# Gates behind the norms in odd MLP blocks, and the first MLP weight in three loads

## Chip, cores, metric

One core of one Trainium2 chip. The metric is the device time of one execution in microseconds. "The span" is the profiled time from the first to the last instruction; it is about 1.8 us shorter than the time of the same run.

## The reference

The result is a gated sum of two branches over 2048 tokens of width 512:

```python
g = sigmoid((x * gate_w).sum(-1, keepdims=True))
a = A(x, mem0, Wq, Wk, Wv, Wo)      # 64 segments of 32 tokens, 32 heads, 8 memory rows carried from segment to segment
y = layernorm(x)
b = gelu(y @ w1 + b1) @ w2 + b2     # w1: 512 x 1376, w2: 1376 x 512
return g * a + (1 - g) * b
```

Only `g` and `b` are touched. The recurrent branch `a` takes the last 87% of the time and stays as it is.

## The kernel before

The kernel computes the whole MLP branch first (about the first 100 us), then the recurrent loop. The 16 tiles of 128 tokens go through the MLP in 8 blocks of two tiles; a block has 11 column blocks `fc` of w1 (ten of 128 columns, one of 96). The loads are queued by SyncE in this order:

```python
ld_x(0, 1); ld_x(1, 2)
nc.sync.dma_start(w1_sb[:, :, 0:3 * P], w1_src[:, :, 0:3 * P])       # 384 KB
ld_x(2, 4)
ld_w2(0, 4)
nc.sync.dma_start(w1_sb[:, :, 3 * P:F], w1_src[:, :, 3 * P:F])       # 992 KB
ld_w2(4, FCF)                                                        # 768 KB
# ... the tail of w2, b2, m0 ...
ld_x(4, 8)                                                           # x of tiles 4 to 7
# ... then Wv, x of tiles 8 to 15, Wq, Wk, Wo
```

`bn(T)` makes mean and variance of a tile on VectorE, `newton` the reciprocal roots, `norm(T)` the normalised tile, `norm_tr(T)` transposes it on TensorE into PSUM bank 7 and copies it out on VectorE (`yT`). `gates(T, T+1)` is the product with `gate_w` and its row sum, on VectorE; `gates2` takes a tanh of the sums on ScalarE and two affine steps on VectorE. `up` is the product with w1 and a GELU on ScalarE; `down` follows two steps later with w2, and its last step evicts the bank (copies it out of PSUM), scaled by `1 - g`:

```python
for u in range(NBLK * FC):
    blk, fc = divmod(u, FC)
    T1 = (blk + 1) * TB                      # first tile of the next block
    pend.append((u, up(u)))
    if fc == 2:
        c_act()                              # ScalarE: eviction of the last block's odd tile, scaled by 1 - g
    if len(pend) > LAG:
        down(*pend.pop(0))                   # at fc == 1 also the VectorE eviction of the last block's even tile
    if T1 < NT:
        if fc == 1 or fc == 3:
            ys[fc // 2] = norm(T1 + fc // 2)
        elif fc == 5 or fc == 7:
            norm_tr(T1 + fc // 2 - 2, ys[fc // 2 - 2])
    if blk % 2 == 0:
        if fc in (2, 5, 6, 7) and T1 + 2 < NT:
            bn(T1 + 2 + (2, 5, 6, 7).index(fc) )
        if fc == 8 and T1 + 2 < NT:
            newton(T1 + 2, T1 + 6)
    elif fc in (2, 4, 6, 8):
        T = T1 + (fc - 2) // 2
        if T < NT:
            gates(T, T + 1)
    elif fc == 10 and T1 < NT:
        gates2(T1, T1 + 4)
    if blk == 0 and fc in (9, 10):
        gates(fc - 9, fc - 8)
    if blk == 1 and fc == 0:
        gates2(0, 2)
    if blk == 1 and fc in (1, 3):
        gates(2 + fc // 2, 3 + fc // 2)
    if blk == 1 and fc == 9:
        gates2(2, 4)
    # ...
```

Instructions of one engine run in this program order. So in block 0 VectorE meets `bn(4)` (at `fc == 2`), which needs the late x load, before `norm(3)`, before the copies of both transposes, and before the gates of tiles 0 and 1.

## Time and profile before

| | |
|---|---|
| time, median of 4 runs | 822.30 us (822.12 to 822.76) |
| profiled run, span | 822.27 us, 820.5 us |
| TensorE idle, whole span | 27.2 us |
| of that, waits between 7.16 and 100 us | 1.18 us for w1, 1.14 us for a GELU |
| first exponential of the recurrent loop | starts at 104.93 us |

How to read it: TensorE has work nearly all the time, so a change pays only if it removes a TensorE wait, or work at half clock, and no later wait grows by as much. The start of the loop's first exponential is a clean mark for that: everything this change can do has happened by then. The views themselves are shown in the prediction.

### The profile page before, as it was taken

How to read it: one execution, taken by the hardware profiler on the slowest of the kernel's cores; microseconds unless marked ns; L12 is line 12 of the kernel's file. 1: busy time of each engine (PE TensorE's matmuls, PEld its weight loads, DVE VectorE, ACT ScalarE, POOL GpSimd, SP SyncE). 2: the span in 40 equal slices, each digit the busy share in tenths (PEclk: the TensorE clock that was granted, in tenths of full speed). 3: DMA queues.
4: the chain of work that ended last, by engine and by line, in shares of the span. 5: the costliest groups of instructions: out<-in, count | busy, mean ns of one | idle time of the engine just before them, and what ended most of it. 6: DMA issues, size and time to landing. Idle time of an engine off the chain costs nothing.

```text
span 820.5 us, 48437 instructions
## 1 busy us (share of the span) xinstructions
PE 793.3 (97%) x22013; PEld 443.2 (54%) x22013; DVE 493.0 (60%) x1022; ACT 446.2 (54%) x1239; POOL 272.1 (33%) x624
## 2 busy tenths in 40 slices
PE   6999999999999999999999999999999999999986
PEld 4666545555555555555555555555555555555543
DVE  5764256565656666665656565656666565656554
ACT  3555545655455555555555655555555556565552
POOL 8100223242434233333424242433333242424220
PEclk9999999999999999999999999999999999999999
DMA  9791310000000010101010100001010101010000
GB/s 315 232 406 53 104 30 10 25 15 17 24 22 25 16 30 10 37 11 36 3 39 8 31 16 22 25 18 28 10 37 10 36 4 41 5 33 8 10 5 24
DMA packets 38357, 37.59 MB, mean 46 GB/s; under 512 B 13561, under 2 KB 36578, under 8 KB 36610
## 3 DMA queue, kind: packets, MB, share of 16 engines
q1 hardware_dynamic: 38018, 34.31, 12.6%
q8 instruction: 174, 2.85, 1.4%
q14 instruction: 37, 0.30, 0.1%
q0 software_dynamic: 128, 0.13, 0.1%
HBM read 26.03 MB, written 6.29 MB: 39 GB/s over the span
## 4 chain that ended last, share of the span: by engine, by line
PE 93%; DVE 3%; DMA 1%; issue 1%; SPq 1%; ACT 1%; DVEq 0%; ACTq 0%
PE b L212 34%; PE b L234 18%; PE b L223 16%; PE b L399 5%; PE b L471 4%; PE b L488 4%; PE b L361 3%; PE b L375 2%; PE b L366 2%; PE b L384 2%; PE b L404 1%; DMA Wo_sb<-in_A_x_dram 1%; PE b L388 0%; DVE R L692 0%; DVE hT L721 0%
## 5 line engine op out<-in xcount | busy, mean ns | idle before, releaser
L218 DVE STREAM_TRANSPOSE Tt<-b 128x512 f32<-128x512 f32 (+1 forms) x384 | 225.6, 613 | 81.6 <-PE b L212 69.0
L212 PEld LDWEIGHTS <-hT 128*32 128x32 bf16 x5120 | 131.0, 97 | 108.5 <-DVE hT L721 23.5
L234 PE MATMUL b<-Wo_sb,UTT 128*32 128x512 bf16 (+1 forms) x2656 | 161.0, 378 | 1.3 <-ACT UTT L763 0.9
L223 PE MATMUL b<-Wv_sb,hT 128*32 128x512 bf16 x2048 | 141.8, 378 | 0.0
L212 PE MATMUL b<-Wq_sb,hT 128*32 128x512 bf16 x2048 | 133.3, 380 | 3.1 <-DVE hT L721 1.7
L212 PE MATMUL b<-Wk_sb,hT 128*32 128x256 bf16 (+1 forms) x3072 | 133.3, 308 | 0.0
L667 ACT CAST KT<-Tt 128x256 bf16<-128x256 f32 (+1 forms) x192 | 87.1, 476 | 53.5 <-DVE Tt L218 53.5
L620 POOL TENSOR_TENSOR Px<-E,R 128x256 bf16<-128x256 bf16 x63 | 42.4, 674 | 209.2 <-DVE R L704 209.2
L704 DVE RECIPROCAL R<-b 128x256 f32<-128x256 f32 x63 | 110.7, 1757 | 0.0
L667 POOL CAST QT<-Tt 128x512 bf16<-128x512 f32 x64 | 39.1, 611 | 187.1 <-DVE Tt L218 187.1
L234 PEld LDWEIGHTS <-UTT 128*32 128x32 bf16 x2656 | 64.4, 96 | 63.7 <-DVE UTT L703 12.1
L711 ACT CAST wsb<-b 128x512 bf16<-128x512 f32 x63 | 36.9, 585 | 111.3 <-PE b L234 111.3
L692 DVE RECIPROCAL R<-b 128x64 f32<-128x64 f32 x63 | 35.1, 557 | 78.6 <-PE b L361 78.6
L634 ACT CAST UTT<-b 128x256 bf16<-128x256 f32 x248 | 74.4, 387 | 9.9 <-PE b L404 8.0
L667 ACT CAST QT<-Tt 128x512 bf16<-128x512 f32 x64 | 39.6, 619 | 68.5 <-DVE Tt L218 68.5
L223 PEld LDWEIGHTS <-hT 128*32 128x32 bf16 x2048 | 49.3, 96 | 21.3
L721 DVE CAST hT<-b 128x32 bf16<-128x32 f32 x63 | 12.0, 191 | 78.8 <-PE b L366 78.8
L476 ACT ACTIVATE hg<-b,b_sb 128x256 bf16<-128x256 f32 x80 | 37.7, 473 | 39.6 <-PE b L471 39.6
L399 PEld LDWEIGHTS <-V 32*128 32x128 bf16 x4064 | 34.4, 91 | 45.5 <-DVE Pm L695 32.2
L471 PE MATMUL b<-yT,w_sb 128*128 128x256 bf16 (+1 forms) x352 | 54.7, 281 | 2.8 <-DMA w_sb<-in_B_w_dram 1.2
L703 ACT CAST UTT<-b 128x64 bf16<-128x64 f32 x126 | 20.6, 215 | 66.1 <-PE b L404 66.1
L622 POOL TENSOR_TENSOR racc<-racc,R 128x320 f32<-128x320 f32 x63 | 54.7, 869 | 0.0
(131 smaller groups left out, 1056.2 us busy)
## 6 DMA issues: line engine op xcount, KB each, us to landing
Wv_sb<-in_A_Wv_dram SPq DMA_DIRECT2D x4, 1024.0 KB
Wq_sb<-in_A_Wq_dram SPq DMA_DIRECT2D x4, 1024.0 KB
Wk_sb<-in_A_Wk_dram SPq DMA_DIRECT2D x4, 1024.0 KB
Wo_sb<-in_A_Wo_dram SPq DMA_DIRECT2D x2, 2048.0 KB
vd<-vt SPq DMA_DIRECT2D x32, 128.0 KB
vs<-vd SPq DMA_DIRECT2D x256, 16.0 KB
out_dram<-o SPq DMA_DIRECT2D x15, 128.0 KB
Wo_sb<-in_A_x_dram SPq DMA_DIRECT2D x1, 1024.0 KB
```

The lines of the kernel that those rows point to most:

```text
L212: nc.tensor.matmul(bk[32 * j:32 * j + 32, 0:n], lhsT=G[:, kc, :], rhs=W5[t][:, kc, h0:h1, j, :], start=(kc == 0), stop=(kc == KC - 1), til ...
L218: nc.vector.transpose(out=Tt[:, 0:n], in_=bk[:, 0:n])
L223: nc.tensor.matmul(bk[32 * j:32 * j + 32, :], lhsT=G[:, kc, :], rhs=Wv5[:, kc, 4 * vb:4 * vb + 4, j, :], start=(kc == 0), stop=(kc == KC - ...
L234: nc.tensor.matmul(bk[32 * g:32 * g + 32, :], lhsT=ut[:, i, j, c0:c0 + 32], rhs=Wo_sb[:, 4 * i + j, d0:d1], start=(j == 0 and i < 4), stop ...
L399: nc.tensor.matmul(U[j][:, i, :], lhsT=V[q, i, :], rhs=Pt[q, i, c_main:c_main + n], start=(i == 0), stop=False, skip_group_check=True, til ...
L471: nc.tensor.matmul(hp[:rows, :], lhsT=w1_sb[:, kc, fc * P:fc * P + rows], rhs=yTs[blk][:, kc, :], start=(kc == 0), stop=(kc == KC - 1))
L476: nc.scalar.activation(out=hg_[:rows, :], in_=hp[:rows, :], func=ACTF.Gelu_apprx_tanh, bias=b1_sb[:rows, fc:fc + 1], scale=1.0)
L620: nc.gpsimd.tensor_tensor(out=Px[:, :, 0:32], in0=E[:, :, 16:48], in1=Rr, op=ALU.mult)
L622: nc.gpsimd.tensor_tensor(out=racc[:], in0=racc[:], in1=R[:], op=ALU.add)
L634: nc.scalar.copy(out=UTT[T % 2][:, :, j, c0 + M:c0 + 40], in_=U[:])
L667: (nc.gpsimd.tensor_copy if bi == 2 else nc.scalar.copy)(out=dst, in_=Tv)
L704: nc.vector.reciprocal(out=R[:, 8 * NG:].rearrange("p (i q) -> p i q", q=32), in_=sr)
```

## The change

The intent: w1's late columns come in two loads, so that the fourth column block need not wait for the last; and in odd blocks the gates stand behind both norms and transposes, so that they can't hold up the next block's input.

```diff
-    nc.sync.dma_start(w1_sb[:, :, 3 * P:F], w1_src[:, :, 3 * P:F])
+    nc.sync.dma_start(w1_sb[:, :, 3 * P:6 * P], w1_src[:, :, 3 * P:6 * P])
+    nc.sync.dma_start(w1_sb[:, :, 6 * P:F], w1_src[:, :, 6 * P:F])
@@ the loop
-        elif fc in (2, 4, 6, 8):
-            T = T1 + (fc - 2) // 2
+        elif fc >= 7:
+            T = T1 + fc - 7
             if T < NT:
                 gates(T, T + 1)
-        elif fc == 10 and T1 < NT:
-            gates2(T1, T1 + 4)
+        if blk % 2 == 0 and blk > 0 and fc == 1:
+            gates2(TB * blk, TB * blk + 4)
@@ block 1
-        if blk == 1 and fc in (1, 3):
-            gates(2 + fc // 2, 3 + fc // 2)
+        if blk == 1 and fc in (5, 6):
+            gates(fc - 3, fc - 2)
```

## The prediction

> **What bounds the kernel now.** I read the page's busy shares and chain first, then busy time by stretch, then the start engine by engine, and last the landing times in the trace.
>
> The page says that TensorE sets the time:
>
> ```profile
> span 820.5 us, 48437 instructions
> PE 793.3 (97%) x22013; PEld 443.2 (54%) x22013; DVE 493.0 (60%) x1022; ACT 446.2 (54%) x1239; POOL 272.1 (33%) x624
> PE 93%; DVE 3%; DMA 1%; issue 1%; SPq 1%; ACT 1%; DVEq 0%; ACTq 0%
> ```
>
> TensorE is idle for 820.5 - 793.3 = 27.2 us in all, 3.3% of the span. The change touches only the MLP stage (the first 100 us), so I asked for TensorE's busy time by stretch there (columns: stretch, its length, busy, granted clock, DMA share, GB/s):
>
> ```profile
> 7.16:10.73 3.57, 3.57 (x14) 1.00 1.05 393
> 10.73:11.91 1.18, 0.00 (x1) 1.00 1.07 389
> 11.91:15.30 3.39, 3.38 (x12) 1.00 1.12 384
> 15.30:23.74 8.44, 8.44 (x63) 1.00 1.01 420
> 23.74:24.89 1.15, 0.01 (x1) 1.00 1.00 401
> 24.89:99.90 75.01, 75.01 (x604) 1.00 0.55 193
> ```
>
> After the first product at 7.16 there are two holes, of 1.18 and 1.15 us; from 24.89 to 99.9 TensorE has no idle time at all. So within the MLP the end moves only if the restart at 24.89 moves. The time line names what each hole waits for:
>
> ```profile
> 11.91 1.03 PE L471 MATMUL b<-yT,w_sb 128*128 128x256 bf16 x4 [1.18 <-DMA w_sb<-in_B_w_dram]
> ...
> 18.15 0.39 PE L460 MATMUL b<-ident,y 128*128 128x128 bf16 x4
> ...
> 24.89 0.60 PE L471 MATMUL b<-yT,w_sb 128*128 128x256 bf16 x4 [1.14 <-ACT hg L476]
> ```
>
> The first hole is the big w1 load, the second is a GELU. ScalarE and VectorE show why that GELU is late:
>
> ```profile
> 16.12 0.69 DVE L414 BATCH_NORM_STATS2 st<-Wo_sb 128x6 f32<-128x512 bf16 x1 [3.72 <-DMA Wo_sb<-in_A_x_dram]
> ...
> 16.95 0.38 DVE L453 TENSOR_SCALAR y<-Wo_sb,mv_all,rstd_all 128x512 bf16<-128x512 bf16 x1
> 17.24 0.42 DVE L461 COPY yT<-b 128x512 bf16<-128x512 bf16 x1
> ...
> 24.16 0.08 DVE L439 DVE_READ_ACCUMULATOR junk<-Wo_sb,gw_bc 128x1 f32 x1
> ```
>
> ```profile
> 24.27 0.20 ACT L442 ACTIVATE th_all<-z_all 128x2 f32<-128x2 f32 x1 [2.13 <-DVE junk L439]
> 24.38 0.82 ACT L476 ACTIVATE hg<-b,b_sb 128x256 bf16<-128x256 f32 x2
> ```
>
> The reader should see one chain: x of tiles 4 to 7 lands at 16.1; VectorE then works without a wait through the statistics of those tiles, the Newton steps and the gates of tiles 0 and 1 until 24.24; the tanh of these gates follows, the GELU stands behind it in ScalarE's order, and TensorE needs that GELU's bank at 24.89. The chain of waits read in order of time agrees: in the first 120 us its longest single piece is
>
> ```profile
> 7.86 8.24 DMA Wo_sb<-in_A_x_dram
> ```
>
> **What the Trainium skill says.** (1) "DMA: Bandwidth & Descriptors", section "Queues, rings and completion order": descriptors of one issuing queue are consumed in ring order on each DMA engine. The trace agrees: SyncE's packets start in order of issue, w1's 1984-byte ones from 7.5 to 11.4, then w2's 1024-byte ones, then x. (2) The same page, "Why small descriptors are slow (HBM only)": each packet carries a fixed overhead. The trace agrees, see below. (3) "TensorE: Matmul & The Clock Gate", section "What's actually happening": the clock is half until a window of about 3.4 us has been busy, and falls back after an idle one. The trace agrees in its durations: starts of 128x256 products are 213 ns apart before 15.30 and 109 ns after it, though the granted clock column reads 1.00 in both. (4) The same page, "Architectural detail: the array is 16× 32×32, not 1× 128×128": ScalarE and VectorE run strictly in order; the GELU behind the tanh agrees.
>
> **The change part by part.**
>
> *w1 in three loads.* The load of columns 384 to 1375 (512 rows of 1984 bytes) becomes 512 rows of 768 and 512 of 1216 bytes. The trace has the old load landing engine by engine from 10.64 to 11.87. A DMA engine has 32 of its packets, at 81 ns each (median) 2.6 us. So on the last engine it starts at about 11.87 - 2.6 = 9.3, and the new first part, 32 packets of about 37 ns = 1.2 us, lands at about 10.5. TensorE issued its last product before the hole at 10.10, and 427 ns later, at 10.53, could have issued the next. So the hole closes: gain there 11.91 - 10.53 = 1.4 us.
>
> It also brings the full clock forward. The switch came at 15.30 after a full busy window from 11.9; the window before it (8.47 to 11.88) was busy for 2.26 of 3.41 us. With the hole closed that one is full and the switch should come at about 11.9. The 3.4 us of half-speed work from there then takes 1.7 us: gain 1.7. Sum at 15.30: about 3.1 us.
>
> How far does it carry? TensorE's next job with an outside dependence is the transpose of tile 3 (the 18.15 row). It needs y of tile 3, which VectorE has at 16.95 + 0.38 = 17.33 because this norm stands behind the first statistics of x tile 4, and the bank that the yT copy frees at 17.24 + 0.42 = 17.66. Reached some 2 to 3 us earlier, it now waits until 17.7. Of the 3.1 us, 18.15 - 17.7 = 0.45 us is left; then 5.6 us of work (18.15 to 23.74) ends at 23.3 instead of 23.74, and the wait for the GELU grows from 1.15 to about 1.6 us. The restart at 24.89 is set by VectorE and the landing of x. Gain at the end: 0.
>
> *Cost of the split.* All packets stand ahead of x tiles 4 to 7 in the same order. Effective time per packet from the windows: 1984 bytes at 413 GB/s is 1984 x 16 / 413 = 76.9 ns; 1024 bytes at 383 GB/s is 42.8 ns; hence 0.0355 ns a byte and 6.4 ns a packet. Estimated from those, 768 + 1216 bytes cost 6.4 ns more than 1984; with 768 bytes as measured in the half microsecond at 335 GB/s (36.7 ns) it is about 9.5 ns. Times 32 packets: 0.2 to 0.3 us later landing, which goes one to one down the chain to 24.89. I take +0.25 us.
>
> *Gates behind the norms, odd blocks.* Nothing is added or removed: 16 gates of 0.685 + 0.08 us, the same tanh and affine steps, only later. In block 1 the norm of tile 4 was done at 25.93 and TensorE transposed it at 27.49 without a wait, so norms earlier gain nothing. The later gates end, by adding six of 0.76 us after the norms and two yT copies, at about 33.4; VectorE's next deadline is the bank eviction at 34.01, where it idled 1.12 us. The gates2 step of an odd block moves behind the next block's first eviction; its consumer is a block away. Cost 0.
>
> Sum: 0 - 0 + 0.25 = +0.25 us, so 822.15 + 0.25 = 822.4 us.
>
> **The rivals.** *The TensorE gain passes through:* 3.1 us off, 819.0 us. For it, the hole at 11.91 is real and the clock would switch earlier; against it, the chain to 24.89 contains no w1 load, only x landing and VectorE. *A new idle stretch cools the clock:* the new wait, about 15.8 to 17.7, could make the gate fall to half speed. A full 3.4 us window at half speed adds 1.7 us to TensorE's 23.3, giving 25.0 against 24.89: about +0.1 to +0.5, so 822.9 us at worst. Against it: an idle of 1.9 us is shorter than the window. *x is issued too late:* SyncE reuses eight DMA slots, and with one load more each request waits on a different earlier one: x tiles 4 to 7 on the landing of x tiles 2 and 3 (7.76) instead of on w1's first part (6.72). It was issued at 7.86 anyway, and its packets are not due before 14.4, so there is slack of some 5 us; the queue held SyncE for 2.6 us at 4.50, so a longer hold is possible. If it slipped by 1 us past the slack: 823.4 us. *The late gates hold an eviction or a tanh:* slack 0.6 us in block 1, so at most a few tenths.
>
> **Range and chances.** Runs before spread over 0.64 us. The terms: -0.5 (an earlier landing that I don't see) to +1. Predicted 822.4 us, 8 in 10 between 821.4 and 823.5. 2% is 16.4 us, over half of all TensorE idle time in the span, so faster 0.005, slower 0.005, within 2% 0.99.
>
> **What would show it.** Right: no wait on w1 at TensorE's fourth column block (it starts near 10.5); full clock near 11.9; a new wait of 1 to 2 us at the transpose of tile 3; the first statistics of x tile 4 starting at 16.3 to 16.5 instead of 16.12; a wait for the GELU of about 1.6 us and restart at 25.1 to 25.2; TensorE without idle from there to 100. Wrong: a restart well before 24.9 (then VectorE or the landing of x was not the limit), a restart after 26 (x issued late), or new holes in blocks 1 to 7 (late gates).

## The result, and the profile after

| | before | changed |
|---|---|---|
| median of 4 runs | 822.30 us (822.12 to 822.76) | 821.91 us (821.30 to 823.10) |
| profiled run, span | 822.27, 820.5 us | 821.30, 819.5 us |
| first exponential of the loop | 104.93 us | 104.82 us |

The ratio is 0.9996, with a 95% interval of 0.9979 to 1.0014: the same. A ratio here is the mean time of one kernel's fast runs over that of the other's of the same rounds, so it isn't quite the ratio of the medians quoted.

The busy shares on the page of the changed kernel:

```profile
span 819.5 us, 48438 instructions
PE 791.6 (97%) x22013; PEld 442.4 (54%) x22013; DVE 493.6 (60%) x1022; ACT 446.4 (54%) x1239; POOL 273.4 (33%) x624
```

TensorE's busy time by stretch in the changed kernel (columns as in the prediction):

```profile
7.15:10.61 3.46, 3.46 (x14) 1.00 1.07 378
10.61:15.79 5.18, 5.18 (x35) 1.00 1.10 383
15.79:17.65 1.86, 0.04 (x2) 1.00 1.01 418
17.65:23.24 5.59, 5.59 (x40) 1.00 1.01 422
23.24:24.78 1.54, 0.00 (x1) 1.00 1.03 419
24.78:99.90 75.12, 75.12 (x604) 1.00 0.55 194
```

The hole for w1 is gone; in its place stand a new one of 1.86 us and a GELU wait that grew from 1.15 to 1.54 us. From the restart to 99.9 there is again no idle time. TensorE's time line says who ends them:

```profile
10.61 1.04 PE L472 MATMUL b<-yT,w_sb 128*128 128x256 bf16 x4
11.44 0.65 PE L489 MATMUL b<-w_sb,hg 128*128 128x512 bf16 x2
11.93 0.60 PE L472 MATMUL b<-yT,w_sb 128*128 128x256 bf16 x4
...
17.65 0.38 PE L461 MATMUL b<-ident,y 128*128 128x128 bf16 x4 [1.82 <-DVE yT L462]
...
24.78 0.60 PE L472 MATMUL b<-yT,w_sb 128*128 128x256 bf16 x4 [1.54 <-ACT hg L477]
```

The fourth column block starts at 10.61 without a wait (11.91 before), the first group wholly at full speed follows at 11.93 (15.30 before), and then TensorE stands at the transpose of tile 3 until VectorE has copied the transpose of tile 2 out of the same bank. VectorE's time line in the changed kernel, with the x load that starts its chain and the first late eviction:

```profile
16.05 0.69 DVE L415 BATCH_NORM_STATS2 st<-Wo_sb 128x6 f32<-128x512 bf16 x1 [3.76 <-DMA Wo_sb<-in_A_x_dram]
...
33.89 0.75 DVE L492 TENSOR_SCALAR c_all<-b,omg_all 128x512 bf16<-128x512 f32 x1 [0.80 <-PE b L489]
```

ScalarE's tanh of the first gates, with the GELUs behind it:

```profile
24.16 0.20 ACT L443 ACTIVATE th_all<-z_all 128x2 f32<-128x2 f32 x1 [2.52 <-DVE junk L440]
24.27 0.82 ACT L477 ACTIVATE hg<-b,b_sb 128x256 bf16<-128x256 f32 x2
```

VectorE's chain starts at 16.05 (16.12 before), the tanh at 24.16 (24.27), and the restart follows at 24.78 (24.89). The gates now fill VectorE up to 33.1, and the eviction at 33.89 still waits for TensorE, not the other way round.

The spans differ by 1.0 us, and it would be easy to credit the change with that. Only 0.11 us of it is there when the loop starts. Lining up the products of the two traces shows two further steps: 0.21 us at 210 us and 0.59 us at 663.5 us. At the second, TensorE of the kernel before paused for nothing that the profile shows; its waits between 657 and 671 us have the line

```profile
PE b L212 <- issue: 0.4, 1, 0.4
```

and the changed kernel's waits there have none such. I take that for scatter of the loop. The changed kernel's four runs spread over 1.8 us, and its two profiles (the second is told of below) differ by 0.43 us at the start of the loop but by 1.73 us in their spans.

### The profile page after: what moved, and what is told of

Same layout as the page of the kernel before. It is cut to its first block, busy times and chain, and to the rows that moved or that the text cites. A ratio compares the mean times of both kernels' runs of the same rounds, so it can differ in the third digit from the quotient of the medians.

```text
span 819.5 us, 48438 instructions
## 1 busy us (share of the span) xinstructions
PE 791.6 (97%) x22013; PEld 442.4 (54%) x22013; DVE 493.6 (60%) x1022; ACT 446.4 (54%) x1239; POOL 273.4 (33%) x624
## 4 chain that ended last, share of the span: by engine, by line
PE 92%; DVE 4%; issue 1%; SPq 1%; DMA 1%; ACT 1%; DVEq 0%; ACTq 0%
PE b L213 33%; PE b L235 18%; PE b L224 16%; PE b L400 5%; PE b L472 4%; PE b L489 4%; PE b L362 3%; PE b L376 2%; PE b L367 2%; PE b L385 2%; PE b L405 1%; DVE R L693 1%; DMA Wo_sb<-in_A_x_dram 1%; DVE Pm L696 1%; PE b L389 0%
```

## The experiments

Theory: the landing of x tiles 4 to 7, and VectorE's chain from there to the tanh of the first gates, set the restart near 24.8 us; the split's gain is real but is waited away behind it; the later gates cost and gain nothing. Rivals: the two parts cancel each other; the change has a small gain that noise hides; the restart doesn't set the end at all.

The table collects all profiles; times in us. "Half speed until" is the start of the last product that took 400 ns or more for 256 columns (or 600 for 512): later ones took 273 (or 379). "Restart" is TensorE's first product after the wait for the GELU. "Loop" is the start of the first exponential.

| kernel | wait for w1 | half speed until | wait at transpose of tile 3 | wait for GELU | restart | loop | median time |
|---|---|---|---|---|---|---|---|
| before | 1.18 | 14.88 | 0 | 1.14 | 24.89 | 104.93 | 822.30 |
| before, second look | 1.82 | 15.69 | 0 | 0.65 | 24.96 | 105.00 | 822.14 (one run) |
| changed | 0 | 11.23 | 1.82 | 1.54 | 24.78 | 104.82 | 821.91 |
| changed, again | 0.53 | 9.56 | 1.70 | 1.56 | 25.21 | 105.25 | 822.60 |
| split only | 0 | 10.13 | 1.81 | 1.51 | 24.94 | 104.99 | 821.84 |
| gates only | 1.75 | 9.43 | 0.70 | 1.54 | 24.74 | 104.78 | 822.18 |
| x earlier | 0 | 10.17 | 0 | 0.49 | 23.34 | 103.38 | 821.03 |
| gates 0, 1 early | 0 | 11.18 | 1.80 | 0 | no wait | 103.44 | 820.52 |
| full reordering | 0.41 | 9.52 | 0 | 0.43 | 23.69 | 101.99 | 818.90 |
| same, one late w1 load | 1.68 | 18.26 | 0 | 0 | no wait | 106.38 | 820.48 |
| same, first look | 1.51 | 9.55 | 0 | 0 | no wait | 102.51 | 819.09 (one run) |
| same, second look | 1.55 | 14.98 | 0 | 0 | no wait | 104.04 | 821.05 (one run) |
| full reordering, old gates | 0 | 10.11 | 0 | 0.41 | 23.52 | 102.45 | 819.61 |
| full reordering, tanh early | 0 | 11.44 | 0 | 0 | no wait | 101.34 | 817.70 |

The times of the kernel before on the chips of these runs had medians of 822.03 (with the first four kernels) and 821.85 us (with the others). All kernels gave the reference's result.

### The changed kernel again

No edit.

> The changed kernel unaltered, to see its spread and a second sample of the landing of x tiles 4 to 7. Theory (the restart near 24.8 us is set by that landing and by VectorE, and the gain of the split is swallowed there): ratio 0.999 to 1.001, no wait on w1, a wait of 1.8 us at the transpose of tile 3 and of 1.5 us for the GELU, restart between 24.7 and 25.2. Rival (a real gain of the change that the first runs hid in noise): ratio below 0.999.

Median of 5: 822.60 us (821.82 to 823.10), ratio 1.0005 (0.9991 to 1.0019). The hidden gain falls. The expectation missed in one place: TensorE waited 0.53 us for w1 here, because that load's first part landed at 11.12 on its last DMA engine, against 10.57 in the first profile. Restart at 25.21, a hair above the stated range.

### The split alone, the gates alone

```diff
 # split only: the kernel before, with
-    nc.sync.dma_start(w1_sb[:, :, 3 * P:F], w1_src[:, :, 3 * P:F])
+    nc.sync.dma_start(w1_sb[:, :, 3 * P:6 * P], w1_src[:, :, 3 * P:6 * P])
+    nc.sync.dma_start(w1_sb[:, :, 6 * P:F], w1_src[:, :, 6 * P:F])
 # gates only: the changed kernel with these three lines the other way round
```

> The three w1 loads alone, gates as before. Theory: TensorE's first 25 us as in the changed kernel (w1 wait gone, clock switch near 11.9, restart 24.7 to 25.2), time within 0.3 us of before. Rival (the split gains and the gates give it back): about 1 to 3 us faster than before, 819 to 821 us.

> The later gates alone, one w1 load as before. Theory: TensorE's holes as in the kernel before (1.2 us for w1, 1.1 us for the GELU), restart near 24.9, no TensorE wait in blocks 1 to 7, time within 0.3 us of before. Rival (late gates cost, split gains): 0.5 us or more slower than before, with a new wait in an odd block or at its end.

Both ratios are 1.0 (0.9987 to 1.0014 each); so neither part gains what the other gives back. TensorE's waits with the split alone:

```profile
17.83 0.38 PE L461 MATMUL b<-ident,y 128*128 128x128 bf16 x4 [1.81 <-DVE yT L462]
...
24.94 0.60 PE L472 MATMUL b<-yT,w_sb 128*128 128x256 bf16 x4 [1.51 <-ACT hg L477]
```

and with the gates alone:

```profile
12.16 0.61 PE L471 MATMUL b<-yT,w_sb 128*128 128x256 bf16 x4 [1.75 <-DMA w_sb<-in_B_w_dram]
...
17.60 0.38 PE L460 MATMUL b<-ident,y 128*128 128x128 bf16 x4 [0.70 <-DVE yT L461]
...
24.74 0.60 PE L471 MATMUL b<-yT,w_sb 128*128 128x256 bf16 x4 [1.54 <-ACT hg L476]
```

The second holds a surprise against the expectation of "holes as in the kernel before": the hole for w1 is there, yet the group after it takes 0.61 us, which is full speed. The clock had switched at about 10 us, ahead of the hole and 5 us earlier than in the first profile of the kernel before, without the split. So the split isn't what decides when the clock switches. And it made no difference: TensorE waited 0.70 us at the transpose and 1.54 us for the GELU, and restarted at 24.74.

### x tiles 4 to 7 earlier

```diff
+    ld_x(4, 8)
     ld_w2(4, FCF)
 ...
-    ld_x(4, 8)
```

> The changed kernel with the load of x tiles 4 to 7 put ahead of the 768 KB of w2. Theory: x lands about 768 KB / 390 GB/s = 2.0 us earlier, VectorE's tanh chain ends 2.0 us earlier, the w2 rows land later and TensorE waits about 1.7 us for them at its fifth down product, the wait for the GELU goes to about zero, and everything from the restart on is 1.8 us earlier: ratio 0.998, about 820.2 us. Rival (the landing of x is not what sets the end, later stages absorb it): no change of the time, ratio 1.000.

Median of 5: 821.03 us (820.20 to 821.98), ratio 0.9988 (0.9975 to 1.0002). The interval alone just fails to exclude no change; the trace decides. TensorE's waits, then VectorE's:

```profile
15.96 0.38 PE L489 MATMUL b<-w_sb,hg 128*128 128x512 bf16 x1 [1.73 <-DMA w_sb<-in_B_w_dram]
...
23.34 0.60 PE L472 MATMUL b<-yT,w_sb 128*128 128x256 bf16 x4 [0.49 <-ACT hg L477]
```

```profile
13.70 0.69 DVE L415 BATCH_NORM_STATS2 st<-Wo_sb 128x6 f32<-128x512 bf16 x1 [1.24 <-DMA Wo_sb<-in_A_x_dram]
...
17.68 0.42 DVE L462 COPY yT<-b 128x512 bf16<-128x512 bf16 x1 [0.81 <-PE b L461]
```

x lands 2.35 us earlier than in the changed kernel's first profile, the restart comes 1.44 us earlier and the loop 1.44 us earlier (104.82 to 103.38): what reaches the restart reaches the loop in full. The wait for w2 of 1.73 us was expected. What I had not counted is that it comes back to VectorE, which now waits 0.81 us for a transpose that TensorE made late; with that the chain to the tanh is longer and 0.49 us of the GELU wait is left.

### Gates of tiles 0 and 1 early

```diff
-        if blk == 0 and fc in (9, 10):
-            gates(fc - 9, fc - 8)
+        if blk == 0 and fc == 1:
+            gates(0, 2)
```

> The changed kernel with the gates of tiles 0 and 1 moved ahead of the statistics of tile 4, into VectorE's idle 12.3 to 16.0. Theory: the tanh no longer waits, the 1.5 us wait for the GELU goes, the 1.8 us wait at the transpose of tile 3 stays: restart point 1.5 us earlier, about 820.4 us, ratio 0.998. Rival (the Newton chain or another consumer of x then holds TensorE at the same place): less than 0.5 us.

Median of 5: 820.52 us (820.40 to 820.79), ratio 0.9983 (0.9969 to 0.9997), as expected. VectorE's idle time before the late x shrinks, and of TensorE's two waits one is left:

```profile
16.37 0.69 DVE L415 BATCH_NORM_STATS2 st<-Wo_sb 128x6 f32<-128x512 bf16 x1 [2.32 <-DMA Wo_sb<-in_A_x_dram]
```

```profile
17.96 0.38 PE L461 MATMUL b<-ident,y 128*128 128x128 bf16 x4 [1.80 <-DVE yT L462]
```

The loop starts at 103.44 although x landed 0.3 us later than in the changed kernel. This shows the tanh behind late gates as the cause of the GELU wait.

### The full reordering

The edit before, and

```diff
-            if fc in (2, 5, 6, 7) and T1 + 2 < NT:
+            if blk == 0:
+                if fc == 5:
+                    bn(4)
+                if fc == 7:
+                    for T in (5, 6, 7):
+                        bn(T)
+            elif fc in (2, 5, 6, 7) and T1 + 2 < NT:
                 bn(T1 + 2 + (2, 5, 6, 7).index(fc) )
```

> As the run before it, and the statistics of tile 4 moved behind TensorE's transpose of tile 2, those of tiles 5 to 7 behind that of tile 3, so that the norms of tiles 2 and 3 and their transposes wait for no later x. Theory: both waits go, all of the split's gain comes through: 1.8 + 1.5 = 3.3 us off the changed kernel, about 818.6 us, ratio 0.996. Rival (the x chain reaches the norm of tile 4 too late, because VectorE starts on x only at 16 us anyway): a wait of 1 us or more at the transpose of tile 4 and 820 us or more.

Median of 5: 818.90 us (818.88 to 819.45), ratio 0.9964 (0.9951 to 0.9978). With 818.9 against the 818.6 expected, 3.0 us off the changed kernel's 821.91 against 3.3 expected, most of what was hidden comes through. Both waits of the changed kernel are gone, and smaller ones show: 0.41 us for w1, 0.30 us for w2, and 0.43 us for a GELU. The last has this cause, on ScalarE and then on TensorE:

```profile
22.59 0.69 ACT L497 ACTIVATE c_all<-b,omg_all 128x512 bf16<-128x512 f32 x1 [0.93 <-DVE omg_all L445]
```

```profile
23.69 0.60 PE L472 MATMUL b<-yT,w_sb 128*128 128x256 bf16 x4 [0.43 <-ACT hg L477]
```

ScalarE's eviction waits for the affine step of gates 0 and 1, which stands behind the Newton steps on VectorE, and the GELUs wait behind the eviction.

### The same with one late w1 load

The full reordering with w1's two late loads as one again, three profiles.

> The same reordering with w1 in two loads as before. Theory: the w1 wait of 1.2 us and the late clock switch at 15.3 are back and are now on the path: about 2.7 to 3.0 us slower than with the split, and 1.1 us faster than before: about 821.2 us, ratio 0.9986. Rival (the split is worth nothing even when it is not hidden): the same time as with the split.

Median of 5: 820.48 us (819.20 to 822.85), ratio 0.9976 (0.9962 to 0.9989). So the split is worth 1.6 us by the medians once nothing hides it, not the 2.7 to 3.0 expected. The spread is the telling part: 3.65 us, against 0.57 us with the split. Two looks were to tell why:

> The full reordering with w1 in two loads once more, for a second sample of when the clock switches: in the first profile the last half-speed product started at 18.26 and the run took 822.85 us, while others of it took 819.2. Theory (the hole for w1 lets the switch fall early or late by the phase of the clock's window, and without the later waits that phase reaches the end): a last half-speed product before 11 goes with about 819.2 to 819.5 us, one at 14 to 15 with about 820.5 to 821, one at 18 with about 822.5. Rival (the spread comes from the loop): no relation.

> The same as the look before it, a third sample, with the same expectations: last half-speed product before 11 with about 819.2 to 819.5 us, at 14 to 15 with about 820.5 to 821, at 18 with about 822.5.

TensorE's group after the hole in the three profiles, first the one that took 822.85 us, then 819.09, then 821.05:

```profile
13.59 1.03 PE L471 MATMUL b<-yT,w_sb 128*128 128x256 bf16 x4 [1.68 <-DMA w_sb<-in_B_w_dram]
```

```profile
12.45 0.61 PE L471 MATMUL b<-yT,w_sb 128*128 128x256 bf16 x4 [1.51 <-DMA w_sb<-in_B_w_dram]
```

```profile
12.66 1.03 PE L471 MATMUL b<-yT,w_sb 128*128 128x256 bf16 x4 [1.55 <-DMA w_sb<-in_B_w_dram]
```

The hole is about the same in all three; the speed after it isn't. Half speed lasted until 18.26, 9.55 and 14.98 us, the loop started at 106.38, 102.51 and 104.04, and the times are in that order, close to the numbers expected for each (the first is the sample from which they were made, so only two test them). The first profile also began late: x of tile 1 came later (its statistics start at 4.35, against 3.79 and 3.77 in the two looks), and the hole ended 1.14 us after that of the 819.09 us run. The rest of its 3.87 us at the loop is the clock: half-speed work from 13.59 to about 19.2 loses half of that, an estimate of 2.8 us; in the third profile 0.21 us and an estimated 1.4 us (12.66 to about 15.4) stand against 1.53 us at the loop. So the cost of the one late load is mostly one of luck: if the clock has switched before the hole, the kernel loses little against the split (one run: 819.09 against 818.90, with the loop 0.52 us later); if not, it works on at half speed for several microseconds.

### The full reordering with the old gates

The full reordering and the split, with the odd blocks' gates as in the kernel before.

> The same reordering with the split, and the odd blocks' gates where they were before the change. Theory: the norms of blocks 1, 3 and 5 have slack, so no TensorE wait and the same time as with the late gates, within 0.3 us: about 818.6 us. Rival (the later gates matter once TensorE runs ahead): a wait at the transpose of tile 4 or 5, and 0.5 us or more slower.

Median of 5: 819.61 us (819.31 to 819.73), ratio 0.9971 (0.9958 to 0.9985); with the late gates 818.90, so they are worth about 0.7 us by the medians. The theory missed here; the rival had the right wait:

```profile
26.97 0.38 PE L461 MATMUL b<-ident,y 128*128 128x128 bf16 x4 [0.46 <-DVE yT L462]
```

TensorE, now earlier, waits at the transpose of tile 5 for the copy of tile 4's, which VectorE reached late behind four gates. The loop starts 0.46 us later than with the late gates (102.45 against 101.99), the size of this wait; I can't assign the rest of the 0.7 us.

### A version that beats both

```diff
                 if fc == 5:
+                    gates2(0, 2)
                     bn(4)
 ...
-        if blk == 1 and fc == 0:
-            gates2(0, 2)
```

> The full reordering with the split and the late gates, and the tanh and affine steps of tiles 0 and 1 moved into block 0, ahead of the statistics of tile 4. In the full reordering ScalarE's eviction of tile 1 waited 0.93 us for the affine step behind the Newton steps, and TensorE then 0.43 us for the GELU behind it. Theory: that wait goes, and the time falls by 0.4 us against the full reordering: about 818.5 us, ratio 0.996. Rival (the norm of tile 4, still behind the Newton steps, then holds TensorE at its transpose): no change, with a wait at the transpose of tile 4.

Median of 6: 817.70 us (816.42 to 818.61), ratio 0.9948 (0.9936 to 0.9961). TensorE's waits in the first 99 us are down to the two at the very start:

```profile
PE b L461 <- DVE y L454: 5.7, 1, 5.7
PE b L472 <- DVE yT L462: 0.5, 1, 0.5
```

The loop starts at 101.34, 0.65 us before that of the full reordering: the GELU wait of 0.43 us is gone, and in this profile there is also no wait for w1 or w2 (0.41 and 0.30 us there), while half speed lasted longer (11.44 against 9.52). The medians differ by 1.2 us, and the two profiled runs, this kernel's the fastest of its six, by 2.5 us. Between these two profiles the rest lies in the loop, mostly in steps of about 0.3 us at products that no edit touched; I don't credit it to the edit.

### The kernel before, looked at again

No edit.

> The kernel before, profiled again. Theory: its clock switch may fall elsewhere than at 15.3, with the restart still at 24.7 to 25.2 and the time within 821.3 to 822.8 us; the later the switch, the shorter the wait for the GELU. Rival (the switch sets the end of the kernel before too): an earlier switch with an earlier restart.

One run, 822.14 us. TensorE in three stretches (columns: stretch, length, busy, granted clock, DMA share, GB/s):

```profile
7.21:10.63 3.42, 3.03 (x14) 1.00 1.05 394
10.63:12.45 1.82, 0.00 (x0) 1.00 1.07 387
12.45:16.10 3.65, 3.65 (x15) 0.53 1.10 390
```

Here the clock switched to full at about 9.3 us, fell back around the hole for w1 and was at half speed again to about 16 (its products of 256 columns took 417 ns). The restart came at 24.96 with a GELU wait of 0.65 us. Within one kernel, later work at half speed shortened the wait and did not move the restart, as the theory has it.

The traces also show what decided the moment. This one's clock records stand at 9.23 (full), 12.64 (half) and 16.06 us (full), 3.41 us apart. Counting back from the first rise in steps of 3.41 us, in all fourteen profiles, TensorE was busy for 80 to 100% of the step just before the rise, and for 76% or less of every step before that. Here it was busy for 35% of the step from 9.23 to 12.64, and the clock fell; later steps of 42 to 49% in other profiles left it at full speed. So where the hole for w1 lies in these steps decides whether it delays the rise; the first microseconds of work are nearly the same from run to run, but the place of the steps isn't.

## Why the prediction was right

It gave 822.4 us (821.4 to 823.5) and the same; measured were 821.91 and, again, 822.60 us. Step by step:

- **The restart as the only point that matters: right.** In six profiles of kernels with the old block 0 (before twice, changed twice, each part alone) it lies between 24.74 and 25.21 us, whatever TensorE did earlier. Moving it (x earlier, gates 0 and 1 early) moved the loop by as much.
- **The hole closes, gain 1.4 us at that place: right.** The fourth column block started at 10.61, against 10.53 worked out, 1.3 us earlier than before. In the second profile it started at 11.17 and 0.53 us of the wait was left.
- **"The switch should come at about 11.9", gain 1.7 us: the number was near, the reason only half of it.** The product at 11.44 took 434 ns, between the 631 of half and the 379 of full speed, and the trace's clock record has the rise at 11.54; 11.93 is the next group. The runs show that the switch moves by itself: without the split, half speed lasted until 9.43, 14.88 and 15.69 us in three profiles. Nor must a window be full: in the second look at the kernel before, the 3.41 us before the rise were busy for 85%, with TensorE's wait of 0.52 us in them. That the switch came near 11.9 was in part luck. My 1.7 us is not what the split gains but what it can gain when the window's phase is bad. Nothing at the end depended on it.
- **New wait at the transpose of tile 3 until 17.7, GELU wait 1.6 us: right**, 17.65 with 1.82 us of wait, and 1.54 us.
- **Cost of the split, +0.25 us: not resolved.** The loads behind the split did land about that much later in the first pair of profiles (the last byte of w1 at 12.16 against 11.87, of w2's second part at 14.32 against 14.06), but x at 16.03 against 16.09. A load counts as landed with its last DMA engine, and from profile to profile that moves more than the term: x's first use lies at 16.01 to 16.17 in three profiles without the split and at 16.05 to 16.45 in the three of the changed kernel and the split alone. The sign may be right; the size is below what these runs can tell. The signs named for it, x's statistics at 16.3 to 16.5 and a restart at 25.1 to 25.2, missed in the first profile (16.05, 24.78), and in the second the statistics came at 16.45 and the restart at 25.21.
- **Late gates, cost 0 and gain 0: right for this kernel.** They ended at 33.1 (33.4 worked out) and the eviction still waited 0.80 us. But "norms earlier gain nothing" holds only while TensorE is held elsewhere; with the waits gone, the late gates saved a wait of 0.46 us.
- **The rivals.** Cooling in the new wait did not happen: the groups after 17.65 took 0.60 us. But the reason given, that 1.9 us is shorter than the window, isn't enough: in the second look at the kernel before a wait of 1.82 us, with one of 0.39 us shortly before it, did bring half speed back. A late issue of x did: SyncE issued it at 9.14 instead of 7.86, well inside the slack, as the prediction reckoned.

## What to carry to other kernels

When a wait near the start is removed, follow the engine to the next thing it needs from outside before counting the gain: here 3 us were won and then waited away, because another load and another engine's in-order work set the restart. A change that measures zero may be worth something together with another one: the order in which VectorE took its work was the lock, and with it opened the same split was worth 1.6 us by the medians (0.2 to 4.0 us by single runs, mostly by the moment of the clock's rise) and the same late gates about 0.5. A term that rests on one profile's moment of a clock switch needs more than one profile.

## What the Trainium skill lacked or had wrong

- "TensorE: Matmul & The Clock Gate", section "What's actually happening", has the clock fall back after an idle window of about 3.4 us. In the second look at the kernel before it fell back around two waits of only 0.39 us (for w2, ending at 10.04) and 1.82 us (for w1, ending at 12.45), with 0.6 us of work between them; the granted clock over the next 3.65 us read 0.53. A later wait of 1.82 us in the changed kernel left it at full speed. The section says that the window is free-running, and these runs agree (half speed lasted until 9.56 and 11.23 us in two profiles of the changed kernel). What it lacks is how much work in a window decides: here 80% or more raised the clock and 76% or less did not, 35% let it fall and 42% or more did not.
- No page warns of it: the granted clock column of the profile reads 1.00 over the half-speed stretch at the start (256-column products 213 ns apart), and shows only a fall back later (0.53). The trace has no clock record before the first rise (15.32 us in the kernel before, 11.54 in the changed one), so at the start the products' own durations must be read.
- "DMA: Bandwidth & Descriptors", section "Where 436 GB/s comes from", says that for transfers between HBM and SBUF the HBM side, about 358 GB/s, binds, though beside it stands a measurement of 425 GB/s. The sentence lacks the condition under which it holds: here, with one core used, the window from 16 to 17 us of the kernel before moved 434 GB/s, and that from 12 to 13 us, with 1 KB packets, 383 GB/s.
- No page has a figure for how far apart the DMA engines finish one load. The first and the last engine of w1's late load in the kernel before finished at 10.64 and 11.87 us, and the last one sets the wait. From profile to profile this moved more (0.4 us at x's first use) than the estimated cost of one more load (0.2 to 0.3 us).
